# Loading the first two float64 weight tiles ahead of expert 1, and taking the low part of the next rows ahead of the row maximum

## The chip, the cores and the metric

One NeuronCore of a Trainium2 chip runs the whole program in one launch. The metric is the device time of one execution in microseconds (us), the median of three runs. Engines: TensorE (PE, matrix products), VectorE (DVE), ScalarE (ACT), GpSimd (POOL, here it issues the gathers) and SyncE (SP, which here only issues DMAs). Each engine takes its instructions in the order in which they are written; semaphores make one engine wait for another.

## The reference

Attention with softmaxed q and k (B 4, H 8, S 576, D 64) gives x of 2304 rows by 512. A mixture of 8 experts picks two experts for each row. A second MLP with a softmax-gated unit and a layer norm follows.

```python
# experts: for each row, its two best experts e with weight g
h = np.maximum(x[mask] @ w1[e], 0.0)            # 512 -> 1024
out[mask] += g * (h @ w2[e])                    # 1024 -> 512
# second MLP, on the 2304 rows that come out
h = x @ w_in                                    # 512 -> 1024
e = np.exp(h - np.max(h, axis=-1, keepdims=True))
sm = e / (np.sum(e, axis=-1, keepdims=True) + 1e-09)
solu = h * sm
ln = (solu - mu) / np.sqrt(var + 1e-06) * g_ln
return (ln @ w_out).astype(np.float32)          # 1024 -> 512
```

w_in and w_out of the second MLP arrive in float64; everything else is float32.

## The kernel before

Every float32 product is made of three matmuls in a reduced-precision type: each operand is split into a high part (a rounded copy, by ScalarE) and a low part (operand minus high part, by VectorE), and high by high, low by high and high by low are added in PSUM.

**The experts.** Each expert gets 640 slots, five tiles of 128 rows. For one expert `e` the program runs eight blocks `mm1(e, m)`, m = 0 to 7, and then five `mm2(e, a)`. A block of `mm1` is 24 matmuls of 320 columns into one PSUM bank `a`, then one ScalarE instruction (L789, `hh`, the high part of the relu) and one VectorE instruction (L790, `hl`, the low part), which is also the last reader of the bank. There are two banks `a`, so the matmuls of block m wait for `hl` of block m - 2. Between the blocks the program writes, in this order, the weights of the next expert (`load_w1`, L157, on SyncE), the rows of the next expert (gather by GpSimd, L736; store, L741; turned read, L747) and one step of a background job `bg`.

**The background job** is a Python generator, `decode_all`, advanced one step by each `next(bg)`. It turns w_in and w_out from float64 words into float32 on VectorE. Its first step only issues two DMAs (`load_f64(0)`, `load_f64(1)`, L204, 512 KB each, into the buffers X0 and X1). Then each of 16 tiles takes four steps: three VectorE instructions (L212 to L214, the first users of the loaded tile), three (L217 to L219), two (L222, L223), and two with the store of the result and the load of the tile after next. In the expert loop one step is taken at each m from 3 to 7 and at each `mm2`.

**The second MLP** handles 18 tiles of 128 rows in turns i. In each turn TensorE does `h_in(i)` (L894, 48 matmuls into a bank `a`, two banks) and then, except in turns 0, 1 and 4, the output product `o_out` of an earlier tile (L986, 24 matmuls of 512 columns). The rest of a turn stands on VectorE and ScalarE: `solu_max(i)` is the row maximum over the bank (L903, VectorE) and the exponential on ScalarE (L906); `solu(i)` (L912 to L919, VectorE) normalizes and is the bank's last reader; `rstd(i - 1)` is a row of small VectorE and ScalarE instructions (L927 to L937). `x2_turn(i + 2)` brings rows to come into transposed order (L870, VectorE) and has ScalarE make their high part `x2h` (L872); `x2_low` takes the low part `x2l` (L877, VectorE) one turn later. `d_low` (L963, VectorE, from turn 4 on) and `d_turn` (L955 on VectorE, L958 on ScalarE) do the same for the second product; for tile 1 the ScalarE copies L976 do it behind `rstd`. `h_in(i + 1)` needs `x2h` in its first matmul and `x2l` in its fifth.

The whole order is the order of the Python code (the schedule is manual), engine by engine.

Of the kernel before, what the change touches and what calls it, by code (L numbers as in the profile page):

```python
# [22 lines left out]
NC = NT // 128  # L23
# [63 lines left out]
def attn_moe_kernel(ctx: ExitStack, tc: tile.TileContext, q, k, v, w_gate, w_noise, noise,  # L87
# [62 lines left out]
    def load_w1(e, j):  # L150
        t = new_raw([128, KD, 256], F32, "raw")
        src = (win32 if e == E else w1[e])[:, 256 * j:256 * j + 256]
        if e < EQ:
            SP.dma_start(out=t, in_=src.rearrange("(k p) f -> p k f", p=128))
        else:
            for g in range(4):
                SP.dma_start(out=t[32 * g:32 * g + 32], in_=src[128 * g:128 * g + 128].rearrange("(k c) f -> c k f", c=32))  # L157
        raw[1, e, j] = t
# [16 lines left out]
    def split_w2(e, j):  # L175
        t = raw.pop((2, e, j))
        if e < E:
            A.copy(W2h[j], t)
            (pick_engine(24 + j, P, V) if e == 0 else V).tensor_sub(W2l[j], t, W2h[j])
        else:  # L180
            wh, wl = W2h[j], W2l[j]
            if j < 2:
                t2 = slot(("XH", "XL")[j], [128, 2, 2, 512], F32R, "w2x")
                wh, wl = t2[:, 0], t2[:, 1]
            WO.append((wh, wl))
            for i in range(2):
                g = gl[:, 2 * j + i:2 * j + i + 1]
                A.activation(out=wh[:, i, :], in_=t[:, i, :], func=AF.Copy, scale=g)
                V.scalar_tensor_tensor(wl[:, i, :], t[:, i, :], g, wh[:, i, :],
                                       op0=OP.mult, op1=OP.subtract)  # L190
# [10 lines left out]
    def load_f64(i):  # L201
        src, _, rs, c0 = dec_src(i)
        t = slot(("X0", "X1")[i % 2], [128, 1024], U32, "f64")
        SP.dma_start(out=t, in_=src[rs, c0:c0 + 512].bitcast(U32))  # L204
        d64[i] = t

    def decode(i):
        _, dst, rs, c0 = dec_src(i)
        t = d64.pop(i).rearrange("p (c w) -> p c w", w=2)
        lw, hw = t[:, :, 0], t[:, :, 1]  # L210
        a, b, c = (slot(tag, [128, 512], U32, f"dec{j}") for j, tag in enumerate((("S5", "S6")[i % 2], "S7", "S11")))
        V.tensor_scalar(b, hw, 3, 0x3FFFFFF8, op0=OP.logical_shift_left, op1=OP.bitwise_and)  # L212
        V.scalar_tensor_tensor(a, hw, 0xC0000000, b, op0=OP.bitwise_and, op1=OP.bitwise_or)
        V.scalar_tensor_tensor(a, lw, 29, a, op0=OP.logical_shift_right, op1=OP.bitwise_or)  # L214
        yield

        V.tensor_scalar(b, lw, 0x1FFFFFFF, 6, op0=OP.bitwise_and, op1=OP.logical_shift_right)  # L217
        V.tensor_scalar(c, a, 0xFF800000, None, op0=OP.bitwise_and)
        V.tensor_tensor(b, b, c, op=OP.bitwise_or)  # L219
        yield  # L220
        af, bf, cf = (x.bitcast(F32) for x in (a, b, c))
        V.tensor_sub(bf, bf, cf)  # L222
        V.scalar_tensor_tensor(af, bf, 2.0 ** -23, af, op0=OP.mult, op1=OP.add)  # L223
        yield

        V.tensor_scalar(c, hw, 20, 0x7FF, op0=OP.logical_shift_right, op1=OP.bitwise_and)
        V.scalar_tensor_tensor(af, c, 896.5, af, op0=OP.is_ge, op1=OP.mult)
        SP.dma_start(out=dst[rs, c0:c0 + 512], in_=af)

    def decode_all():  # L230
        load_f64(0)
        load_f64(1)
        yield
        for i in range(16):
            yield from decode(i)
            if i < 14:
                load_f64(i + 2)
            yield
# [493 lines left out]
    def gather_x(e, a):  # L732
        c = E * a + e
        t = (new_row if e < EQ else new_hop)([128, DM], F32, "xg")
        first = e == 0 and a < TA
        P.indirect_dma_start(out=t, out_offset=None, in_=xd[0:NRA, :] if first else xd, in_offset=bass.IndirectOffsetOnAxis(  # L736
            ap=idxA[:, a:a + 1] if first else idx[:, c:c + 1], axis=0))
        xg[e, a] = t

    def write_x(e, a):  # L740
        SP.dma_start(out=xs_d[e, a], in_=xg[e, a])  # L741
# [34 lines left out]
    def mm1(e, m):  # L776
        hi, lo = XT[e]
        pa = bank_a()
        j, o = m // 2, 128 * (m % 2)
        for n in range(2):  # L780
            for kk in range(KD):
                wh, wl = W1h[j][:, kk, o:o + 128], W1l[j][:, kk, o:o + 128]
                xh, xl = hi[:, kk, HC * n:HC * n + HC], lo[:, kk, HC * n:HC * n + HC]
                for s, (a, b) in enumerate(((wh, xh), (wh, xl), (wl, xh))):
                    T.matmul(pa[:, n, 0:HC], lhsT=a, rhs=b, start=(kk == 0 and s == 0),  # L785
                             stop=(kk == KD - 1 and s == 2))
        h, l = h_tiles(m)
        h2, l2 = (x.rearrange("p (n c) -> p n c", n=2) for x in (h, l))
        A.activation(out=h2, in_=pa[:, :, 0:HC], func=AF.Relu)  # L789
        V.scalar_tensor_tensor(l2, pa[:, :, 0:HC], 0.0, h2, op0=OP.max, op1=OP.subtract)  # L790
# [68 lines left out]
    def x2_read(t):  # L859
        x = x2r[t] = new_raw([128, 2, DM], F32, "xq")  # L860
        for g in range(4):
            SP.dma_start(out=x[32 * g:32 * g + 32, 0].rearrange("i (b f) -> i b f", b=4),  # L862
                         in_=xx[t].rearrange("(b i) f -> i b f", i=32)[:, :, 128 * g:128 * g + 128])
# [11 lines left out]
    def x2_low(t):  # L875
        hi, lo, xt = x2T[t]
        V.tensor_sub(lo, xt, hi)  # L877
        x2T[t] = (hi, lo)
# [82 lines left out]
    def d_low(t):  # L961
        hi, lo, xt = dT[t]
        V.tensor_sub(lo, xt, hi)  # L963
        dT[t] = (hi, lo)
# [188 lines left out]
    def load_gl():  # L1153
        for g in range(4):
            SP.dma_start(out=gl[32 * g:32 * g + 32], in_=g_ln[256 * g:256 * g + 256].rearrange("(k c) -> c k", c=32))
# [31 lines left out]

    load_gl()
    bg = decode_all()
    for e in range(1, E):  # L1190
        for m in range(KF):
            mm1(e, m)
            if m < 4:
                split_w2(e, m)
                load_w1(e + 1, m)
            if e + 1 < E and m < NA:
                gather_x(e + 1, m)
            if EQ <= e + 1 < E:
                if 1 <= m < NA + 1:
                    write_x(e + 1, m - 1)  # L1200
                if 3 <= m:
                    read_x(e + 1, m - 3)
            if m >= 3:
                next(bg, None)
            if e == 2 and m == 5:
                pair_gates()
                count_overflow()
        if stop:
            return
        for a in range(NA):  # L1210
            if e + 1 < E:
                xt_tile(e + 1, a)
            mm2(e, a)
            if e < E - 1:
                next(bg, None)
                if a < 4:
                    split_w1(e + 1, a)
                    load_w2(e + 1, a)
                continue
            gather_y(a)  # L1220
            if a < 2:
                for j in (2 * a, 2 * a + 1):
                    split_w1(E, j)
                    load_w2(E, j)
            elif a == 2:
                next(bg, None)
                combine(0)
                split_w2(E, 0)
            elif a == 3:
                x2_trans(0)  # L1230
                combine(1)
                split_w2(E, 1)
# [7 lines left out]
    for i in range(NC + 3):  # L1240
        if i < NC:
            h_in(i)
        if i == 1:
            d_trans(0)
        if NP <= i - 1 < NC - 2:
            d_read(i - 1)
        if 1 <= i < NC - 2:
            x2_read(i + 2)
        if i < NC:
            solu_max(i)  # L1250
        if NP <= i - 2 < NC - 2:
            d_low(i - 2)
        if 2 <= i < NC - 1:
            x2_low(i + 1)
        if i < NC:
            solu(i)
        if NP <= i < NC - 2:
            d_write(i)
        if i == 0:
            x2_trans(2)  # L1260
        if i < NC - 3:
            combine(i + 3)
        if i == 1:
            split_w2(E, 3)
        if 1 <= i <= NC:
            rstd(i - 1)
        if 2 <= i < 2 + NP:
            o_out(i - 2)
        if i >= 3 + NP:
            o_out(i - 3)  # L1270
        if i in (NP, NC - 1, NC):
            d_trans(i - 1)
        if NP <= i - 1 < NC - 2:
            d_turn(i - 1)
        if 1 <= i < NC - 2:
            x2_turn(i + 2)
        if i + 5 < NC:
            gather_y(i + 5)
# [31 lines left out]
```

## Time and profile before

| what | value |
|---|---|
| time, median of 3 runs | 799.62 us (799.24 to 801.07) |
| the profiled execution | 799.58 us, of which its span (first to last instruction) 797.8 us |
| TensorE busy | 743.6 us, 93% of the span |
| VectorE / ScalarE / GpSimd busy | 67% / 37% / 18% |
| mean granted TensorE clock | 0.975 of full speed |
| mean DMA rate | 180 GB/s |

The span is divided by time: attention and routing up to some 110 us, expert 0 to 179 us, experts 1 to 7 to 582 us, the second MLP to the end. TensorE is busy nearly throughout from expert 1 on, so its few gaps there, and the stretches at a lower granted clock, are where time can be found or lost. The granted clock has two levels here, 1.00 (2.4 GHz) and 0.50 (1.2 GHz). In a timeline row the bracket tells how long the engine sat idle before the instruction and who ended that.

### The profile page before, as it was taken

The numbers are of one execution on the slowest core, as the hardware profiler recorded it, in microseconds if no ns is written. First come the engines' busy times: TensorE is split into PE (matmuls) and PEld (weight loads), VectorE is DVE, ScalarE is ACT, GpSimd is POOL, SyncE is SP. The second block draws the span as 40 slices with busy tenths as digits, with TensorE's granted clock in tenths as the row PEclk, the third lists the DMA queues.
The fourth block names the chain that finished last, engine by engine and source line by source line (L and its number), as shares of the span: only waits on it lengthen the run. The fifth ranks groups of instructions, "written<-read, shape, count | busy, mean of one in ns | idle before, by whom it ended". The sixth has DMA issues, their size and how long they took to land. (4 is left out here: it accounts for less than half of the span.)

```text
span 797.8 us, 12649 instructions
## 1 busy us (share of the span) xinstructions
PE 743.6 (93%) x4754; PEld 670.1 (84%) x4754; DVE 532.2 (67%) x929; ACT 298.7 (37%) x489; POOL 144.8 (18%) x130
## 2 busy tenths in 40 slices
PE   2877877999699999999999999999999899999997
PEld 1776866989689989889889899899898898899986
DVE  6999784244475876776766766765467878777771
ACT  1556551233033233233233333233345544454441
POOL 3684375100100200201101101000344211100000
PEclk9998799999799999999999999999999999999999
DMA  9973363446745865965847848542747776655411
GB/s 276 280 241 107 120 198 106 146 133 161 207 159 163 241 207 153 267 211 158 251 146 217 245 158 234 176 132 80 211 132 231 233 221 215 192 180 182 149 40 40
DMA packets 115280, 143.60 MB, mean 180 GB/s; under 512 B 19856, under 2 KB 80784, under 8 KB 115216
## 3 DMA queue, kind: packets, MB, share of 16 engines
q1 hardware_dynamic: 109136, 122.83, 50.4%
q0 software_dynamic: 6080, 19.93, 8.9%
q8 instruction: 38, 0.62, 0.3%
q14 instruction: 26, 0.21, 0.1%
HBM read 99.46 MB, written 43.25 MB: 179 GB/s over the span
## 5 line engine op out<-in xcount | busy, mean ns | idle before, releaser
L785 PE MATMUL a<-xh,w1h 128*128 128x320 f32 x448 | 139.9, 312 | 6.9 <-DVE hl L790 6.9
L785 PE MATMUL a<-xl,w1h 128*128 128x320 f32 x448 | 139.6, 312 | 0.0
L785 PE MATMUL a<-xh,w1l 128*128 128x320 f32 x448 | 139.6, 312 | 0.0
L821 PE MATMUL b<-w2h,hl 128*128 128x512 f32 x320 | 126.8, 396 | 0.0
L821 PE MATMUL b<-w2l,hh 128*128 128x512 f32 x320 | 126.4, 395 | 0.0
L821 PE MATMUL b<-w2h,hh 128*128 128x512 f32 x320 | 126.3, 395 | 0.0
L736 POOL DMA_INDIRECT xg<-xd,idx x38 | 39.5, 1040 | 327.7 <-DMA xs<-xg 317.7
L789 ACT ACTIVATE hh<-a 128x640 fp32r<-128x640 f32 x56 | 39.5, 706 | 153.3 <-PE a L785 153.3
L790 DVE SCALAR_TENSOR_TENSOR hl<-a,hh 128x640 fp32r<-128x640 f32 x56 | 46.2, 824 | 74.8 <-ACT hh L789 74.8
L785 PEld LDWEIGHTS a<-xh,w1h 128*128 128x128 f32 x448 | 85.3, 190 | 7.5 <-DVE hl L790 7.1
L785 PEld LDWEIGHTS a<-xl,w1h 128*128 128x128 f32 x448 | 85.3, 190 | 0.4
L785 PEld LDWEIGHTS a<-xh,w1l 128*128 128x128 f32 x448 | 85.2, 190 | 0.0
L821 PEld LDWEIGHTS b<-w2l,hh 128*128 128x128 f32 x320 | 60.1, 188 | 14.1
L821 PEld LDWEIGHTS b<-w2h,hh 128*128 128x128 f32 x320 | 60.2, 188 | 13.8
L821 PEld LDWEIGHTS b<-w2h,hl 128*128 128x128 f32 x320 | 60.0, 188 | 13.9
L844 POOL DMA_INDIRECT yg<-yd,posi x36 | 36.6, 1017 | 166.1 <-DVE w1l L173 72.9
L894 PE MATMUL a<-w1h,x2l 128*128 128x256 f32 x288 | 57.9, 282 | 2.5 <-DVE x2l L877 2.5
L894 PE MATMUL a<-w1h,x2h 128*128 128x256 f32 x288 | 58.1, 283 | 0.7 <-DVEq L1003 0.5
L894 PE MATMUL a<-w1l,x2h 128*128 128x256 f32 x288 | 57.2, 280 | 0.0
L771 ACT CAST xh<-xt 128x512 fp32r<-128x512 f32 x30 | 18.6, 621 | 94.5 <-DVE xt L769 94.5
L986 PE MATMUL b<-w2x,dT 128*128 128x512 f32 x216 | 53.5, 396 | 0.1
L986 PE MATMUL b<-w2h,dT 128*128 128x512 f32 x144 | 48.0, 395 | 0.0
(216 smaller groups left out, 1377.0 us busy)
## 6 DMA issues: line engine op xcount, KB each, us to landing
raw<-in_moe_w_dram SPq DMA_DIRECT2D x40, 512.0 KB, 3.9
raw<-in_moe_w_dram SPq DMA_DIRECT2D x96, 128.0 KB, 3.0
yd<-yo SPq DMA_DIRECT2D x40, 256.0 KB, 2.1
xs<-xg SPq DMA_DIRECT2D x30, 256.0 KB, 4.2
xg<-xs SPq DMA_DIRECT2D x120, 64.0 KB, 4.4
dd<-ed SPq DMA_DIRECT2D x14, 512.0 KB, 2.6
dq<-dd SPq DMA_DIRECT2D x56, 128.0 KB, 3.1
k<-in_k_dram SPq DMA_DIRECT2D x4, 1024.0 KB, 7.0
```

The source lines that it names most:

```text
L736: P.indirect_dma_start(out=t, out_offset=None, in_=xd[0:NRA, :] if first else xd, in_offset=bass.IndirectOffsetOnAxis(ap=idxA[:, a:a + 1] ...
L771: A.copy(hi, x)
L785: T.matmul(pa[:, n, 0:HC], lhsT=a, rhs=b, start=(kk == 0 and s == 0), stop=(kk == KD - 1 and s == 2))
L789: A.activation(out=h2, in_=pa[:, :, 0:HC], func=AF.Relu)
L790: V.scalar_tensor_tensor(l2, pa[:, :, 0:HC], 0.0, h2, op0=OP.max, op1=OP.subtract)
L821: T.matmul(pb, lhsT=x, rhs=y, start=(kk == 0 and s == 0), stop=(kk == KF - 1 and s == 2))
L844: P.indirect_dma_start(out=r, out_offset=None, in_=yd[0:n, :], in_offset=bass.IndirectOffsetOnAxis(ap=posi[:, c, j:j + 1], axis=0))
L894: T.matmul(pa[:, n, 256 * c:256 * c + 256], lhsT=x[:, kk, :], rhs=w[2 * n + c][:, kk, :], start=(kk == 0 and s == 0 and c == 0), stop=(kk ...
L986: T.matmul(pb, lhsT=x[:, kk, :], rhs=w, start=(kk == 0 and s == 0), stop=(kk == KF - 1 and s == 2))
```

## The change

It makes two edits. The first takes the first step of `bg` (the two float64 loads) ahead of the expert loop and leaves out the step at m = 3 of expert 1, so that from m = 4 of expert 1 on every step stands where it stood. The second writes `x2_low(i + 1)` ahead of `solu_max(i)` in the turns of the second MLP; it stood behind `solu_max(i)` and `d_low(i - 2)`.

```diff
     load_gl()
     bg = decode_all()
+    next(bg)
     for e in range(1, E):
...
-            if m >= 3:
+            if m >= 3 + (e == 1):
                 next(bg, None)
...
         if 1 <= i < NC - 2:
             x2_read(i + 2)
+        if 2 <= i < NC - 1:
+            x2_low(i + 1)
         if i < NC:
             solu_max(i)
         if NP <= i - 2 < NC - 2:
             d_low(i - 2)
-        if 2 <= i < NC - 1:
-            x2_low(i + 1)
         if i < NC:
             solu(i)
```

SyncE's instructions, from the end of expert 0 to m = 5 of expert 1, as a difference (f are the float64 tiles, raw the weights of expert 2, xg and xs its rows; a number behind xs_ is the tile).

```order
 L824 DMA yd<-yo 128x512 x3
 L1155 DMA gl<-in_moe_g_ln_dram 32x8x1 x4
+L204 DMA f_1843<-in_moe_w_in_dram 128x1024
+L204 DMA f_1845<-in_moe_w_in_dram 128x1024
 L157 DMA raw<-in_moe_w_dram 32x4x256 x8
 L741 DMA xs_0_95<-xg 128x512
...
 L747 DMA xg<-xs_0_95 32x4x128 x4
-L204 DMA f_1995<-in_moe_w_in_dram 128x1024
-L204 DMA f_1997<-in_moe_w_in_dram 128x1024
 L741 DMA xs_3_98<-xg 128x512
 L747 DMA xg<-xs_1_96 32x4x128 x4
```

The two loads now stand ahead of all weight loads and row transfers of expert 2 that are issued during expert 1.

VectorE's instructions at the start of turn 4 of the second MLP, before (dq and dT are d's tile and its parts, a is the bank of `h_in(4)`):

```order
L955 STREAM_TRANSPOSE dq<-dq 128x4x8x32
L870 STREAM_TRANSPOSE xq<-xq 128x4x4x32
L903 TENSOR_REDUCE col<-a 128x1
L963 TENSOR_TENSOR dT<-dq,dT 128x1024
L877 TENSOR_TENSOR x2l<-xq,x2h 128x512
L912 TENSOR_SCALAR col<-col 128x1
```

And the same place now:

```order
L955 STREAM_TRANSPOSE dq<-dq 128x4x8x32
L870 STREAM_TRANSPOSE xq<-xq 128x4x4x32
L877 TENSOR_TENSOR x2l<-xq,x2h 128x512
L903 TENSOR_REDUCE col<-a 128x1
L963 TENSOR_TENSOR dT<-dq,dT 128x1024
L912 TENSOR_SCALAR col<-col 128x1
```

The subtraction L877 has moved up past the maximum L903 and, from turn 4 on, past L963; in turns 2 and 3 it has moved past L903 alone.

## Rows read from the trace of the kernel before

**Rows 1.** Waits of TensorE: waiting instruction <- releaser: us in total, times, longest.
```profile
PE a L785 <- DVE hl L790: 6.9, 1, 6.9
...
PE a L894 <- DVE x2l L877: 2.5, 2, 2.2
```

**Rows 2.** VectorE's timeline, expert 1: start, us, engine, instruction [idle before].
```profile
196.36 0.82 DVE L790 SCALAR_TENSOR_TENSOR hl<-a,hh 128x640 fp32r<-128x640 f32 x1 [1.36 <-ACT hh L789]
206.81 0.43 DVE L212 TENSOR_SCALAR dec<-f 128x512 uint32<-128x512 uint32 x1 [9.63 <-DMA f<-in_moe_w_in_dram]
...
208.60 0.81 DVE L790 SCALAR_TENSOR_TENSOR hl<-a,hh 128x640 fp32r<-128x640 f32 x1
```

**Rows 3.** SyncE's timeline: DMA issues from the end of expert 0.
```profile
179.03 2.35 SPq L1155 DMA_DIRECT2D gl<-in_moe_g_ln_dram  x4
184.47 5.26 SPq L157 DMA_DIRECT2D raw<-in_moe_w_dram  x8
...
200.70 0.90 SPq L204 DMA_DIRECT2D f<-in_moe_w_in_dram  x2
```

**Rows 4.** TensorE's timeline, the matmul after the wait of expert 1.
```profile
209.47 0.63 PE L785 MATMUL a<-xh,w1h 128*128 128x320 f32 x1 [6.86 <-DVE hl L790]
```

**Rows 5.** Windows: TensorE busy, its granted clock (PEclk), DMA share, GB/s.
```profile
210.00:215.00 5.00, 5.00 (x21) 0.50 0.67 191
```

**Rows 6.** ScalarE's timeline, first matmul of expert 1.
```profile
199.14 0.71 ACT L789 ACTIVATE hh<-a 128x640 fp32r<-128x640 f32 x1 [2.82 <-PE a L785]
202.66 0.70 ACT L789 ACTIVATE hh<-a 128x640 fp32r<-128x640 f32 x1 [2.81 <-PE a L785]
216.01 0.71 ACT L789 ACTIVATE hh<-a 128x640 fp32r<-128x640 f32 x1 [12.64 <-PE a L785]
```

**Rows 7.** TensorE's timeline, turn 5 of the second MLP.
```profile
625.81 0.50 PE L894 MATMUL a<-w1h,x2h 128*128 128x256 f32 x2 [0.16 <-ACT x2h L872]
...
628.70 0.80 PE L894 MATMUL a<-w1h,x2l 128*128 128x256 f32 x2 [2.16 <-DVE x2l L877]
...
635.43 2.96 PE L986 MATMUL b<-w2x,dT 128*128 128x512 f32 x12
```

**Rows 8.** VectorE's timeline, turn 2 of the second MLP.
```profile
606.58 1.19 DVE L903 TENSOR_REDUCE col<-a 128x1 f32<-128x1024 f32 x1
607.68 0.67 DVE L877 TENSOR_TENSOR x2l<-xq,x2h 128x512 fp32r<-128x512 f32 x1
609.03 0.15 DVE L912 TENSOR_SCALAR col<-col 128x1 f32<-128x1 f32 x1 [0.68 <-ACT ed L906]
```

**Rows 9.** ScalarE's timeline, the high part of tiles 3 and 5.
```profile
606.69 0.62 ACT L872 CAST x2h<-xq 128x512 fp32r<-128x512 f32 x1 [1.87 <-DVE xq L870]
...
625.15 0.61 ACT L872 CAST x2h<-xq 128x512 fp32r<-128x512 f32 x1
```

**Rows 10.** VectorE's timeline, turn 4.
```profile
625.69 1.22 DVE L903 TENSOR_REDUCE col<-a 128x1 f32<-128x1024 f32 x1 [0.94 <-PE a L894]
...
627.97 0.68 DVE L877 TENSOR_TENSOR x2l<-xq,x2h 128x512 fp32r<-128x512 f32 x1
```

**Rows 11.** TensorE's timeline, end of turn 3's first matmul.
```profile
613.47 0.40 PE L894 MATMUL a<-w1h,x2l 128*128 128x256 f32 x2
```

**Rows 12.** The chain that ended last, in order of time: start, us, what.
```profile
614.00 6.10 PE b L986 x24
620.09 5.58 PE a L894 x48
...
646.72 5.55 PE b L986 x24
```

**Rows 13.** TensorE's timeline, a wait of expert 0.
```profile
117.30 0.39 PE L809 MATMUL a<-xh,w1h 128*128 128x256 f32 x1 [2.05 <-DVE hl L812]
```

**Rows 14.** VectorE's timeline, turn 6.
```profile
646.75 1.23 DVE L903 TENSOR_REDUCE col<-a 128x1 f32<-128x1024 f32 x1 [1.78 <-PE a L894]
```

**Rows 15.** ScalarE's timeline, the high part of tile 7.
```profile
645.37 0.62 ACT L872 CAST x2h<-xq 128x512 fp32r<-128x512 f32 x1
```

## Prediction

> **What bounds the kernel now.** The table of the profile says that TensorE is busy for 93% of the span, so I read first what it waits for. The view of waits, TensorE alone, has two entries behind expert 0 that are worth a microsecond [rows 1]: once 6.9 us in the experts' first product, for VectorE's `hl`, and 2.5 us in two pieces in the second MLP, for `x2l`. The reader should see the counts: these are single events and no steady cost. What the one event is made of stands in the timelines of that place. The lower level of the granted clock shows in windows, and the chain that ended last shows that from 635 us on there is only TensorE, one `h_in` and one `o_out` in turn, so that a microsecond won ahead of that point is won at the end.
>
> The first event: VectorE finishes `hl` of block 4 at 197.2 us, then sits idle for 9.63 us at the background job's first instruction, because the float64 tile has not landed [rows 2]. SyncE issued that load only at 200.70 [rows 3], behind the weights and rows of expert 2. The `hl` of block 5 stands behind the waiting instruction in VectorE's order and comes at 208.60 [rows 2], so the bank for block 7 is not free and TensorE waits 6.86 us [rows 4]. After the wait the granted clock is 0.50, the lower of its two levels [rows 5], so the block runs slowly too.
>
> **The first edit, step by step.** It adds nothing: the same two loads, earlier. SyncE is done with the small loads L1155 at 181.4 and issues nothing until 184.47, where the weight loads wait for their buffers [rows 3]. The two issues take 0.90 us, so they fit in that gap and push nothing back. The first tile was needed 6.1 us after its issue last time (200.70 to 206.81) [rows 2, 3]; from about 181.5 that gives 187.6, or 193 at double the time, and VectorE asks for it at 197.2. So the wait of 9.63 us goes completely. Moving 1 MB out of the busiest stretch also cannot hurt the row transfers that are issued there.
>
> What is late next? In the place of the wait VectorE has the first decoding step, 1.8 us (206.81 to 208.60), ending at 199.0, and `hh` of block 5 starts at 199.14 [rows 2, 6]. `hl` of block 5 then ends near 200.7, ahead of block 7's start at about 202.5. So TensorE doesn't wait at all. Blocks come 3.52 us apart (199.14 to 202.66), so `hh` of block 7 moves from 216.01 to 202.66 + 3.52 = 206.18 [rows 6]. **That is 9.83 us**: 6.86 of waiting, and 2.97 of a block at the lower clock. Behind it, the transposes of expert 2's rows come 10 us sooner, yet their turned reads are issued from 198 us on and get ahead of the need by more than they did, and the other background steps move with TensorE. I take the whole 9.83; the lower bound, if only the idle time counted, is 6.86, the upper one 9.83.
>
> **The second edit, step by step.** It adds no instruction; it moves a subtraction of 0.67 us [rows 8]. The place aimed at is turn 4: `x2h` of tile 5 is ready at 625.76 [rows 9], but `x2l` only starts at 627.97, behind the maximum (which waits for `h_in(4)`) and `d_low` [rows 10]. TensorE waits 2.16 us for it and runs slowly afterwards: `h_in(5)` takes from 625.81 to 635.43 [rows 7], 9.62 us, against 5.58 in [rows 12]. Taken alone, with `x2l` done at 626.45, it would lose only some 0.2 us and end at 631.6: a gain of 3.8.
>
> But in turns 2 and 3 the move costs VectorE time, and there VectorE, not TensorE, sets the pace. In turn 2 the maximum starts at 606.58, `x2l` fills the time in which ScalarE makes the exponential, and L912 comes at 609.03, 2.45 us after the maximum's start, still with 0.68 idle ahead of it [rows 8]. So `x2l` is free today. Now it stands first and must wait for `x2h`, which ScalarE ends at 607.31 [rows 9]; it runs from 607.34 to 608.0, the maximum starts there and L912 follows 2.45 us later. Turn 2 becomes 1.4 us later: 0.7 of waiting, 0.7 of a subtraction that has lost its cover. Turn 3 has the same instructions in the same relation, and loses another 1.4. (If `x2h` were ready in time, each would lose 0.67: the other bound.)
>
> What hangs on that? `rstd(1)`, then ScalarE's dT copies, then `o_out(1)`: from 614.00 to 615.4 [rows 12]. TensorE has nothing ahead of it, as `h_in(3)` is done at about 613.9 [rows 11]. `o_out(1)` and `h_in(4)` take 6.1 and 5.6 [rows 12], to 627.1. `x2h` of tile 5 comes 2.8 late, 625.15 becoming 627.95, and ends at 628.56 [rows 9]; `x2l` follows at once, to 629.3. `h_in(5)` starts at 628.6, needs the low part after four matmuls, waits 0.2, and has 44 matmuls left. At full clock those take 5.58 x 44 / 48 = 5.12 us, so it ends at 634.4 instead of 635.43 [rows 7, 12]. **The second edit gives 1.0 us**, not 3.8: the wait of 2.16 for `x2l` is largely replaced by a wait of 1.5 for `x2h`.
>
> Afterwards VectorE must not become the bound. From turn 6 on it sat idle for 1.78 us ahead of the maximum [rows 14], which began at 646.75; it was therefore done with the transpose at 644.97. `x2h` ends at 645.99 [rows 15], so 1.02 of waiting and some 0.6 for the subtraction (to the next issue) fit into the 1.78. Behind the maximum the subtraction's place is saved in part. So TensorE keeps its pace, and VectorE works off what it is late.
>
> **Sum.** 799.58 (the profiled execution, 0.04 below the median) - 9.83 - 1.0 = 788.75, say 788.8.
>
> **The clock in the ramp.** The new plan leaves TensorE idle for about 1.5 us twice (613.9 to 615.4, 627.1 to 628.6). Today a wait of 2.16 us in turn 5 ended with slow matmuls: 44 of them took 628.70 to 635.43, 6.73 us [rows 7], 1.6 more than the 5.12; but a wait of 2.05 us in expert 0 was followed by a matmul of 0.39 us, hardly slower than later ones [rows 13]. So the rows allow both. A fall in the first gap costs nothing, since it only fills the second one; one in the second gap costs up to 1.6. By the Trainium skill (TensorE: Matmul & The Clock Gate, What's actually happening), the array returns to the half clock when it has not been busy, and how many matmuls that slows varies from run to run. That would speak for the rival below, 790.4; the rows above show it once and deny it once, so I keep it as a rival.
>
> **Rivals.**
> 1. The clock falls in the second gap. `h_in(5)` then ends at 629.3 + 6.73 = 636.0, 0.6 later than now: 799.58 - 9.83 + 0.6 = 790.4.
> 2. The ramp hides the subtraction's new place (`x2h` ready, or the maximum waiting for TensorE anyway). Then the second edit gives between 2.6 (0.67 lost in each turn) and 3.8: 786.0 to 787.1. Against it: the maximum of turn 2 shows no idle time ahead of it [rows 8].
> 3. The first stall is only passed on: VectorE waits for expert 2's rows instead, and part of the 9.83 is lost, down to 6.86 or less: 791.7 to 797. For it: DMA is busy there, 0.67 in [rows 5]. Against it: SyncE issues that stretch's transfers no later than before.
> 4. Slower: the second edit puts VectorE's turn over TensorE's 11.1 us (5.6 + 5.6 [rows 12]) in the steady turns. From the point where `x2h` comes more than 0.2 us later than in [rows 15] and the saving behind the maximum doesn't make up for it, every turn pays; to eat both gains (10.8 us) the 12 turns behind would have to pay 0.9 us each; at 1.0 the time is 788.8 + 12 = 800.8. Against it: 1.78 against 1.62.
> 5. The loads don't come sooner, because the DMAs ahead of them hold SyncE: no change, 799.6 less at most 1.
>
> **How the numbers follow.** The forecast has 0.55 (788 to 789.6), rival 1 0.20, rival 2 0.10, rival 3 0.08, rival 5 0.03, rival 4 0.04. The range 786.0 to 791.5 holds the first three and the best of the fourth, and takes in both bounds of the turn's cost. About 0.2% (1.6 us) is what a measurement of this kernel can tell from no change; the forecast and rivals 1 to 3 lie beyond it: faster 0.93, the same 0.03, slower 0.04.
>
> **What would show it.** The loads L204 at about 181.5; no VectorE idle at L212 in expert 1; TensorE without the wait at block 7, clock 1.00 throughout; `mm2` of expert 1 starting at 206 instead of 215.8. In the second MLP, about 10 us earlier than now: idle time ahead of `x2l` in turns 2 and 3, the maximum 1.4 later in turn 2; `o_out(1)` waiting 1.5 us; `h_in(5)` waiting for `x2h` rather than `x2l`, and ending about 10.8 us ahead of 635.43. Wrong would be: a wait for the rows of expert 2 on TensorE, or waits in every turn behind turn 6.

## The result, and the profile after

The changed kernel takes **789.56 us** (median of 4 runs, 788.43 to 790.55) where the kernel before took 799.43 on the same chip (4 runs, 797.77 to 801.07): a ratio of 0.9876 [0.985, 0.9903], 9.9 us less. 788.8 was predicted. The profiled execution takes 790.4 us, its span 788.6.

**The loads.** SyncE's timeline around the end of expert 0 (start, us, instruction):

```profile
180.42 2.31 SPq L1155 DMA_DIRECT2D gl<-in_moe_g_ln_dram  x4
182.78 0.92 SPq L204 DMA_DIRECT2D f<-in_moe_w_in_dram  x2
185.86 5.26 SPq L157 DMA_DIRECT2D raw<-in_moe_w_dram  x8
```

The two loads stand right behind L1155, 15.7 us ahead of the step that first needs them. The weights come at 185.86 where they came at 184.47 [rows 3]. That is 1.39 us later, but so is everything: the first `hh` of expert 1 starts at 182.93 and started at 181.54. The loads push nothing back. VectorE's timeline, where the wait of 9.63 us stood [rows 2]:

```profile
197.75 0.82 DVE L790 SCALAR_TENSOR_TENSOR hl<-a,hh 128x640 fp32r<-128x640 f32 x1 [1.36 <-ACT hh L789]
198.49 0.49 DVE L212 TENSOR_SCALAR dec<-f 128x512 uint32<-128x512 uint32 x1
...
201.27 0.82 DVE L790 SCALAR_TENSOR_TENSOR hl<-a,hh 128x640 fp32r<-128x640 f32 x1 [0.84 <-ACT hh L789]
```

L212 follows with no idle time, and `hl` of block 5 now waits for ScalarE, so VectorE has time left. ScalarE's timeline, the last three `hh` of expert 1:

```profile
200.53 0.71 ACT L789 ACTIVATE hh<-a 128x640 fp32r<-128x640 f32 x1 [2.81 <-PE a L785]
204.05 0.70 ACT L789 ACTIVATE hh<-a 128x640 fp32r<-128x640 f32 x1 [2.81 <-PE a L785]
207.57 0.70 ACT L789 ACTIVATE hh<-a 128x640 fp32r<-128x640 f32 x1 [2.82 <-PE a L785]
```

Blocks come 3.52 us apart to the end; the last two stood 13.35 apart [rows 6]. The windows (TensorE busy, PEclk, DMA share, GB/s at the end of the row) show TensorE without a gap and at full clock in expert 1, and at full clock to the end:

```profile
176.00:216.00 40.00, 40.00 (x245) 37.70 (x244) 21.08 (x29) 11.55 (x15) 4.70 (x5) 1.00 0.84 228
...
570.00:788.00 218.00, 210.28 (x1349) 188.26 (x1347) 153.90 (x308) 101.63 (x190) 31.66 (x30) 1.00 0.53 166
```

**The second MLP.** VectorE in turns 2, 3 and 4 (`x2l` L877, the maximum L903, L912):

```profile
598.98 0.71 DVE L877 TENSOR_TENSOR x2l<-xq,x2h 128x512 fp32r<-128x512 f32 x1 [0.69 <-ACT x2h L872]
599.61 1.21 DVE L903 TENSOR_REDUCE col<-a 128x1 f32<-128x1024 f32 x1
602.09 0.15 DVE L912 TENSOR_SCALAR col<-col 128x1 f32<-128x1 f32 x1 [1.27 <-ACT ed L906]
...
609.62 0.69 DVE L877 TENSOR_TENSOR x2l<-xq,x2h 128x512 fp32r<-128x512 f32 x1 [0.69 <-ACT x2h L872]
610.23 1.22 DVE L903 TENSOR_REDUCE col<-a 128x1 f32<-128x1024 f32 x1
...
620.24 0.69 DVE L877 TENSOR_TENSOR x2l<-xq,x2h 128x512 fp32r<-128x512 f32 x1 [1.04 <-ACT x2h L872]
620.85 1.22 DVE L903 TENSOR_REDUCE col<-a 128x1 f32<-128x1024 f32 x1
```

In turn 2 VectorE stands idle for 0.69 us ahead of `x2l`, which then runs ahead of the maximum, and the idle time ahead of L912 has grown from 0.68 [rows 8] to 1.27: the subtraction has lost its cover. I count from the start of `h_in(0)`, 582.85 before and 574.43 now. The maximum of turn 2 moves from 23.73 to 25.18, that of turn 3 to 35.80 from 32.96: 1.45 and then another 1.39 late. TensorE's timeline shows what hangs on it:

```profile
607.05 3.30 PE L986 MATMUL b<-w2x,dT 128*128 128x512 f32 x12 [0.53 <-ACT dT L976]
...
620.26 0.51 PE L894 MATMUL a<-w1h,x2h 128*128 128x256 f32 x2 [1.56 <-ACT x2h L872]
...
620.99 0.51 PE L894 MATMUL a<-w1h,x2l 128*128 128x256 f32 x2
...
626.26 2.96 PE L986 MATMUL b<-w2x,dT 128*128 128x512 f32 x12
```

`h_in(5)` waits 1.56 us for `x2h` and hardly for `x2l` any more (2.16 in [rows 7]), and `o_out(2)` starts 51.83 us behind `h_in(0)`; before it was 52.58 (635.43 - 582.85). So the edit won 0.75 us there. In the view of TensorE's waits (us in total, times, longest) L785 has no row, and the second MLP's products have these, beside 0.5 us ahead of `h_in(0)` that was there before too:

```profile
PE a L894 <- ACT x2h L872: 1.6, 1, 1.6
PE b L986 <- issue: 1.3, 2, 0.9
...
PE b L986 <- ACT dT L976: 0.5, 1, 0.5
```

The wait for `hl` (6.9) and that for `x2l` (2.5) of [rows 1] are gone.

**Where the time went, in one sum.** The spans differ by 9.2 us (797.8 - 788.6). From the first `hh` of expert 1 to that of its last block it is 34.47 before and 24.64 now, 9.83 less; from there to `h_in(0)` 366.84 and 366.86, the same; from `h_in(0)` to the end 214.95 and 214.17, 0.78 less; and up to expert 1, which the change doesn't touch, 1.39 more. 9.83 + 0.78 - 1.39 = 9.22.

### The profile page after: what moved, and what is told of

Same layout as the page of the kernel before. It is cut to its first block, busy times and chain, and to the rows that moved or that the text cites. A ratio compares the mean times of both kernels' runs of the same rounds, so it can differ in the third digit from the quotient of the medians.

```text
span 788.6 us, 12651 instructions
## 1 busy us (share of the span) xinstructions
PE 742.2 (94%) x4754; PEld 668.5 (85%) x4754; DVE 531.4 (67%) x929; ACT 298.9 (38%) x489; POOL 145.2 (18%) x130
## 5 line engine op out<-in xcount | busy, mean ns | idle before, releaser
L785 PE MATMUL a<-xh,w1h 128*128 128x320 f32 x448 | 138.6, 309 | 0.0
L785 PE MATMUL a<-xh,w1l 128*128 128x320 f32 x448 | 138.5, 309 | 0.0
L785 PE MATMUL a<-xl,w1h 128*128 128x320 f32 x448 | 138.5, 309 | 0.0
L785 PEld LDWEIGHTS a<-xl,w1h 128*128 128x128 f32 x448 | 84.2, 188 | 0.4
L785 PEld LDWEIGHTS a<-xh,w1h 128*128 128x128 f32 x448 | 84.2, 188 | 0.3
L785 PEld LDWEIGHTS a<-xh,w1l 128*128 128x128 f32 x448 | 84.3, 188 | 0.0
L986 PEld LDWEIGHTS b<-w2x,dT 128*128 128x128 f32 x216 | 39.3, 188 | 10.8 <-issue 1.8
```

Source lines behind the costliest of these rows:

```text
L986: T.matmul(pb, lhsT=x[:, kk, :], rhs=w, start=(kk == 0 and s == 0), stop=(kk == KF - 1 and s == 2))
```

## The experiments

The runs are in three groups, each on one chip with its own runs of the kernel before: the first four of the table behind the kernels shown, the next four, and the last two. Because the part ahead of expert 1 differs by up to 3.2 us from one execution to the next, the profiles are compared by the two stretches of that sum: **A**, first to last `hh` of expert 1's first product, and **B**, `h_in(0)` to the end. The stretch between them is 366.84 to 366.88 us in all twelve profiles. The medians of the kernel before in the three groups are 796.26, 796.98 and 798.25 us; the two rows "before again" are single executions.

| kernel | A | B | time, us | ratio to before |
|---|---|---|---|---|
| before, as shown | 34.47 | 214.95 | | |
| after, as shown | 24.64 | 214.17 | 789.56 | 0.9876 [0.985, 0.9903] |
| loads alone | 24.64 | 213.53 | 788.81 | 0.9908 [0.9883, 0.9934] |
| low part alone | 34.59 | 213.87 | 796.53 | 1.0002 [0.9985, 1.0018] |
| early place from turn 4 | 24.63 | 211.41 | 785.25 | 0.9867 [0.984, 0.9893] |
| before, wait filled | 31.38 | 214.67 | 795.14 | 0.9981 [0.9964, 0.9998] |
| early place in turns 2, 3 | 24.64 | 219.51 | 792.83 | 0.9933 [0.9908, 0.9958] |
| loads at m = 2 | 24.64 | 214.67 | 789.61 | 0.9905 [0.9877, 0.9933] |
| before again | 32.46 | 215.04 | 796.11 | |
| before again | 33.26 | 213.29 | 796.09 | |
| after again | 24.63 | 214.34 | 789.85 | 0.9876 [0.984, 0.9912] |
| early place in turn 4 alone | 24.63 | 214.26 | 787.37 | 0.9841 [0.9805, 0.9876] |

The theory is the prediction's: the loads give 9.83 us, the moved subtraction wins 3.8 in turn 4 and pays 2.8 in turns 2 and 3. The rivals are that turns 2 and 3 pay nothing, and that a part of the first gain is the clock's and not the wait's.

**The first edit alone.**

```diff
     bg = decode_all()
+    next(bg)
...
-            if m >= 3:
+            if m >= 3 + (e == 1):
```

> The two early loads alone, the subtraction where it was. Theory of the prediction: 9.83 us less than before, 789.8, and in the second MLP the same waits as before, 2.16 us for x2l in turn 5 with slow matmuls behind it. Rival (the second edit is what gains, or the first stall is passed on): less than 8 us gained, with a new wait on TensorE between block 7 of expert 1 and expert 2.

A is 24.64, as in the changed kernel, so the whole of A's gain is this edit's. By time it gives 7.45 us (796.26, 23 runs, to 788.81, 6 runs); its interval, 5.3 to 9.3 us, does not reach 9.83. It is less than the 8 us that the rival named, but the rival's sign, a new wait of TensorE, isn't there: the stretch behind A is 366.87. A second thing was not expected. The chain that ended last has `h_in(5)`'s last 44 matmuls behind the same wait of 2.16 us for `x2l`:

```profile
618.45 5.44 PE a L894 x44
```

They take 5.44 us, at full clock, where the same chain of the kernel before has 6.89. The wait was the same to 0.01 us, and the clock did not fall.

**The second edit alone.**

```diff
         if 1 <= i < NC - 2:
             x2_read(i + 2)
+        if 2 <= i < NC - 1:
+            x2_low(i + 1)
         if i < NC:
             solu_max(i)
...
-        if 2 <= i < NC - 1:
-            x2_low(i + 1)
```

> The early subtraction alone, the loads where they were. Theory: 0.75 to 1.0 us less than before, 798.6 to 798.9; the maximum of turn 2 starts 1.4 us later against h_in(0) than before, that of turn 3 2.7 later, and h_in(5) waits about 1.6 us for x2h instead of 2.2 for x2l. Rival (the ramp hides the new place of the subtraction, and what held the second edit back was something of the shifted program, such as the pause in o_out(0)): 2.6 to 3.8 us less, 795.8 to 797.

The time doesn't change: 796.53 against 796.26, 1.0002 [0.9985, 1.0018], between 1.2 us won and 1.4 lost. The mechanism is there all the same. VectorE's timeline of turn 2:

```profile
607.34 0.69 DVE L877 TENSOR_TENSOR x2l<-xq,x2h 128x512 fp32r<-128x512 f32 x1 [0.69 <-ACT x2h L872]
607.95 1.22 DVE L903 TENSOR_REDUCE col<-a 128x1 f32<-128x1024 f32 x1
```

and TensorE's waits:

```profile
PE a L785 <- DVE hl L790: 7.4, 1, 7.4
PE b L986 <- ACT dT L976: 1.8, 1, 1.8
PE a L894 <- ACT x2h L872: 1.6, 1, 1.6
```

The prediction's two waits of 1.5 us are these 1.8 and 1.6. In the changed kernel the first is only 0.5, because there TensorE had already lost 1.3 us in front of it ("issue" in its view of waits; more on that below).

**Early from turn 4 on, old place in turns 2 and 3** (both edits, without the part of the second that should cost).

```diff
+        if 4 <= i < NC - 1:
+            x2_low(i + 1)
         if i < NC:
             solu_max(i)
         if NP <= i - 2 < NC - 2:
             d_low(i - 2)
-        if 2 <= i < NC - 1:
+        if 2 <= i < 4:
             x2_low(i + 1)
```

> Both edits, but the subtraction goes ahead of the maximum only from turn 4 on; in turns 2 and 3 it stands behind it as before. Theory (turns 2 and 3 each lose 1.4 us and eat most of the 3.8 that turn 4 gains): 3.8 us less than with the loads alone, 786.0, with h_in(5) waiting less than 0.5 us in all and the clock at 1.00 there. Rival (the early place costs in turn 4 and after, not in turns 2 and 3): the time of the changed kernel or more, 788.8 and above.

This is the fastest of its group, 785.25 us (5 runs, 784.87 to 786.31), 3.6 less than the loads alone (787.02 to 790.11); the runs of the two don't overlap. B is 211.41: 3.54 less than in the profile of the kernel before, against 3.8 in the prediction, and 2.76 less than in that of the changed kernel, against 2.8. Both are differences between two executions, and against the profile of the loads alone, where the clock did not fall, it is 2.12. TensorE has one wait for `x2l` in the second MLP, and its timeline shows where:

```profile
597.71 0.51 PE L894 MATMUL a<-w1h,x2l 128*128 128x256 f32 x2 [0.33 <-DVE x2l L877]
```

That is `h_in(3)`, where the kernel before waited 0.30 us too (the smaller of the two pieces of 2.5 in [rows 1]). In `h_in(5)` no wait is left in the view. VectorE, turn 2 and turn 4:

```profile
595.88 1.19 DVE L903 TENSOR_REDUCE col<-a 128x1 f32<-128x1024 f32 x1
596.98 0.67 DVE L877 TENSOR_TENSOR x2l<-xq,x2h 128x512 fp32r<-128x512 f32 x1
...
615.08 0.69 DVE L877 TENSOR_TENSOR x2l<-xq,x2h 128x512 fp32r<-128x512 f32 x1 [1.04 <-ACT x2h L872]
615.69 1.21 DVE L903 TENSOR_REDUCE col<-a 128x1 f32<-128x1024 f32 x1
```

In turn 2 the maximum covers `x2h`'s 0.69 us and ScalarE's exponential covers the subtraction; in turn 4 `x2l` is first and delays nothing on which TensorE waits.

**The kernel before, with matmuls in the wait.** 46 matmuls on old operands, into a bank that nobody reads, ahead of block 7: the wait stays, only the clock is kept up.

```diff
+    def fill(n):
+        ps, x = bank_t(), XT[1][0]
+        for _ in range(n):
+            T.matmul(ps[:, 0:HC], lhsT=W1h[0][:, 0, 0:128], rhs=x[:, 0, 0:HC], start=True, stop=True)
...
+            if e == 1 and m == 7:
+                fill(46)
             mm1(e, m)
```

> The kernel before, with 46 added matmuls of 320 columns (6.75 us at full clock) into an unused bank ahead of block 7 of expert 1, so that TensorE is busy while VectorE waits for the float64 tile. They compute nothing that is read. Theory (the slow block is TensorE's own idling): granted clock 1.00 through block 7, which takes 3.5 us instead of 6.4; the time falls by 2.97 us at most, to 796.7, although work was added. Rival (the clock falls there for another reason, such as the busy DMA queues): block 7 stays slow, and the time is 799.6 or a little more.

TensorE's timeline and the window of the stretch (PEclk third from the end):

```profile
201.82 6.91 PE L1193 MATMUL t<-xh,w1h 128*128 128x320 f32 x46
```

```profile
180.00:216.00 36.00, 36.00 (x237) 35.28 (x237) 17.43 (x23) 9.77 (x13) 4.73 (x5) 1.00 0.72 200
```

Block 7 ran at full clock and A fell by 3.09 us, so the slow block went with TensorE's idling, and 6.74 us beyond the 24.64 were left, the wait with the added matmuls in it. By time it gave 1.1 us (0.2 to 2.9 by the interval): less than 2.97, but the interval takes in 2.3, the mean slow block of the four profiles below. In this execution the clock fell in turn 5 (44 matmuls in 6.93 us), as before.

The loads alone and this run both gave less than the profile before had promised. How much do wait and slow block vary, then, from one execution of the kernel before to the next? **The kernel before, twice more, unchanged:**

> The kernel before once more, for its profile. If the clock behind a wait varies from run to run, the wait of block 7 is 6 to 7.5 us again, while the slow part of block 7 costs anything between 0.5 and 3 us and h_in(5) takes 7.9 us (full clock behind the wait for x2l) or 9.6. If it does not vary, block 7 ends 9.8 us late and h_in(5) takes 9.6 again.

> The kernel before a third time, for the same two readings as the second.

TensorE behind the wait in the first, and the window behind it:

```profile
207.39 0.64 PE L785 MATMUL a<-xh,w1h 128*128 128x320 f32 x1 [6.28 <-DVE hl L790]
```

```profile
208.00:210.00 2.00, 2.00 (x10) 2.00 (x9) 1.97 (x4) 0.00 (x0) 1.05 (x2) 0.50 0.34 96
210.00:212.00 2.00, 2.00 (x15) 2.00 (x15) 0.75 (x2) 0.00 (x0) 0.88 (x1) 0.94 0.88 226
```

and in the second:

```profile
208.46 0.63 PE L785 MATMUL a<-xh,w1h 128*128 128x320 f32 x1 [6.41 <-DVE hl L790]
```

```profile
210.00:212.00 2.00, 2.00 (x9) 2.00 (x9) 1.82 (x3) 0.00 (x0) 1.67 (x2) 0.50 0.63 136
212.00:214.00 2.00, 2.00 (x13) 2.00 (x12) 0.00 (x0) 0.00 (x0) 0.04 (x1) 0.80 0.94 245
```

The wait is 6.28 and 6.41, but the clock comes back some 3 us behind its end in the one and some 4 in the other, where [rows 5] show it low for at least the 5 us to 215. A beyond the 24.64 without the wait is 7.82 and 8.62. With the 9.83 of [rows 6] and the 9.95 of the low part alone, four profiles give 7.8 to 10.0, 9.06 in the mean, of which the slow block is 1.5 to 3.0. The execution on which the prediction was built had the largest slow block of the four. In turn 5, too, the clock fell in one of the two (B 215.04) and not in the other (213.29).

**The early place in turns 2 and 3 alone** (loads early, `2 <= i < 4` ahead of `solu_max`, the rest at the old place), to measure their cost by itself.

> The loads early, and the subtraction ahead of the maximum in turns 2 and 3 alone; from turn 4 on behind maximum and d_low as before. Theory (turns 2 and 3 lose 1.3 to 1.4 us each, and turn 4 gains): x2l of turn 4 starts 2.0 us later against h_in(0) than with the loads alone, TensorE loses 1.6 us ahead of h_in(5) for x2h and 1.4 inside it for x2l; from h_in(0) to o_out(2) 53 us, against 51.3 measured with the loads alone and 49.2 with the early place from turn 4 on. Rival (the early place costs nothing in turns 2 and 3): 51.3.

`o_out(2)` starts 57.14 us behind `h_in(0)`, later than either theory expected, and the time is 792.83. The same reading gives 51.16 with the loads alone and 49.01 with the early place from turn 4 on. TensorE's timeline, and VectorE's maximum of turn 4:

```profile
590.84 0.29 PE L894 MATMUL a<-w1l,x2h 128*128 128x256 f32 x1 [0.81 <-issue]
...
621.07 0.79 PE L894 MATMUL a<-w1h,x2l 128*128 128x256 f32 x2 [2.47 <-DVE x2l L877]
```

```profile
618.06 1.23 DVE L903 TENSOR_REDUCE col<-a 128x1 f32<-128x1024 f32 x1 [1.26 <-issue]
```

The wait for `x2l` of turn 4 is 2.47 us now and is followed by slow matmuls (44 in 8.1 us). But TensorE also paused in `h_in(2)` with no releaser, and `o_out(0)` starts 2.8 us later than in the kernels without such a pause (21.04 behind `h_in(0)` against 18.16 to 18.23). That reached `x2l` as well: VectorE stood idle for 1.26 us ahead of the maximum of turn 4, which began when the late `h_in(4)` ended. `x2l` started 48.34 us behind `h_in(0)`, 3.20 later than with the loads alone (45.14); take off the 1.26, and an estimate of 1.94 is left, where the theory said 2.0. How much of the 57.14 is the pause's is not measured, so the run gives the sign of the cost, and its size only by that estimate.

**The loads one block earlier only** (the step at m = 3 taken at m = 2), to see how early is early enough.

```diff
-            if m >= 3:
+            if m >= 3 + (e == 1) or (e == 1 and m == 2):
```

> The two loads one block earlier than before, at m = 2 of expert 1 instead of m = 3, and no second edit. Theory (the stall follows the landing of the float64 tile one for one): the issue moves from 200.7 to about 197.2, the wait of TensorE from 6.86 to 3.4 us, and with or without slow matmuls behind it the time is 3.5 to 6.5 us less than before. Rival (the stall is set by the queue of row transfers, in which the loads only change places): the wait stays at 6 us or more.

SyncE's timeline, and then VectorE's:

```profile
194.14 0.97 SPq L204 DMA_DIRECT2D f<-in_moe_w_in_dram  x2
```

```profile
199.87 0.43 DVE L212 TENSOR_SCALAR dec<-f 128x512 uint32<-128x512 uint32 x1 [2.31 <-DMA f<-in_moe_w_in_dram]
```

A miss on the place: the issue came at 194.14, since in SyncE's order it stands ahead of the transfers of m = 3. The tile lands at 199.87, and VectorE waits 2.31 us for it, but TensorE not at all (A 24.64). So it is not necessary that VectorE's wait goes: the bank has at least that much to spare. The ratio is that of the loads alone (0.9905 and 0.9908).

**The changed kernel again, and the early place in turn 4 alone** (`i == 4`; all other turns old), on a third chip. The first run asks what the second edit adds to the loads, the second whether the steady turns need it.

> The changed kernel again, beside the next one on one chip. Theory as the runs so far leave it (the second edit ends h_in(5) at a fixed 51.5 to 52 us after h_in(0), where the old order ends it at 51.2 or 52.6 as the clock falls or not): the time within 1 us of the loads alone, a ratio to before near 0.990; h_in(0) to the end 213.9 to 214.2 us. Rival (the second edit gains the 1.0 us of the prediction on top in every run): 0.9865 to 0.988.

> The loads early and the subtraction ahead of the maximum in turn 4 alone, in all other turns behind it. Theory (turn 4 is the only place where the early subtraction is worth anything): h_in(0) to the end 211.4 us as with the early place from turn 4 on, 2.2 to 2.8 us less than the changed kernel, ratio to before near 0.986. Rival (the steady turns need the early place too): more than 212 us from h_in(0) to the end, with waits for x2l behind turn 5.

The changed kernel gives 0.9876 [0.984, 0.9912], which holds both answers: not settled by time. B is 214.34, a little above what was expected. Turn 4 alone has 0.9841 [0.9805, 0.9876]; its interval overlaps that of "from turn 4 on", so these two are not told apart either. By the medians it is 2.5 us faster than the changed kernel beside it (787.37 and 789.85), as expected, but the runs overlap. Its waits in the second MLP, and the window behind the first of them (PEclk third from the end):

```profile
PE b L986 <- issue: 2.2, 3, 1.0
...
PE a L894 <- issue: 0.3, 1, 0.3
```

```profile
598.00:600.00 2.00, 2.00 (x7) 0.50 0.23 71
```

B was expected at 211.4 and is 214.26 in this profile. The 2.2 us of pause in `o_out(0)` and the slow matmuls behind it are 2.20 of the difference: `o_out(2)` starts 51.21 us behind `h_in(0)`, against 49.01 with the early place from turn 4 on. Most of the rest, 0.6 us, is the row of 0.3, which the view gives no releaser. It is the fifth matmul of `h_in(6)`, the first to need `x2l` of tile 6, and VectorE's subtraction had ended 0.06 us ahead of it:

```profile
632.17 0.51 PE L894 MATMUL a<-w1h,x2l 128*128 128x256 f32 x2 [0.32 <-issue]
```

```profile
631.43 0.68 DVE L877 TENSOR_TENSOR x2l<-xq,x2h 128x512 fp32r<-128x512 f32 x1
```

So turn 5, with its subtraction at the old place, was late by 0.3 us in this execution, as the rival says. Behind it no matmul waits for `x2l` or `x2h`: the turns from 6 on don't need the early place.

## Why the prediction was right, and which term was off

- **The wait for the tile, and what takes its place:** right. The wait is gone, nothing is late next, `hh` of block 7 comes 9.83 us sooner, and the stretch up to the second MLP is unchanged to 0.04 us in every profile. The rivals that it would be passed on (3) or that the loads would not come sooner (5) are refuted.
- **The size of the first term:** 9.83 was one execution's. The wait of 6.86 was 6.3 to 7.4 in four profiles, and the 2.97 of slow block was 1.5 to 3.0. The mean of the four is 9.06; the loads alone measured 7.45 [5.3, 9.3] by time, which holds 9.06 and not 9.83.
- **Turns 2 and 3, 1.4 us each:** right, 1.45 and 1.39. That the first turns hide the subtraction's new place (rival 2) is refuted by the profiles of the changed kernel and of the low part alone: `x2l` waits 0.69 for `x2h` with the maximum behind it.
- **Turn 4, 3.8 alone and 1.0 net:** right as a mechanism: 3.54 alone, 2.76 paid, 0.78 net against the execution that it was worked out from. `h_in(5)` starts 45.83 us behind `h_in(0)`; 45.75 was forecast.
- **The step that failed** is the price of the old wait in turn 5: "`h_in(5)` takes from 625.81 to 635.43 [rows 7], 9.62 us" was taken as what it costs always. In six profiles that have the old order in turn 4 with no pause ahead, the clock fell behind that wait in four (B 214.67, 214.67, 214.95, 215.04) and not in two (213.29, 213.53); the mean is 214.36. The three profiles with the second edit, two of them with a pause that the last section tells of, have 213.87, 214.17 and 214.34, mean 214.13. So **the second edit gives 0.2 us by these means, where 1.0 was predicted**: 0.7 won (214.83 - 214.13) when the clock would have fallen, 0.7 lost (213.41) when it would not. With six and three profiles the 0.2 is not clear of nothing. The timed run of that edit alone (1.0002) agrees, though its interval just holds a gain of 1.0 us. A part of the spread is another wait: in eight of the twelve profiles VectorE waited 0.2 to 0.4 us ahead of L870 in turn 2 (0.35 before, 0.41 in the changed kernel). In the four where it did not, B is 214.67 and 214.67 with the clock fallen and 213.29 without in the old order, and 213.87 with the second edit alone: 0.8 won or 0.6 lost.
- **The clock in the second gap (rival 1):** it stayed up behind the 1.56 us of the changed kernel and the 1.58 of the low part alone. The Trainium skill (TensorE: Matmul & The Clock Gate, What's actually happening) says that how many matmuls come slow varies between runs of one kernel; the rows agree and go further: behind 2.14 to 2.16 us of idle the 44 matmuls took 6.89 to 6.97 us in four executions, and 5.44 and 5.46, with no fall of the clock, in two.
- **VectorE in the steady turns (rival 4):** refuted. The subtraction waits 1.04 or 1.05 us for `x2h` in each (1.02 forecast), and no matmul waits behind turn 5.
- **The total** came out closer than its terms: 9.06 + 0.23 = 9.3 by the profiles' means, 10.8 predicted, 9.9 measured with an interval from 7.7 to 12.0. The two edits timed each alone add up to less still, 7.45 - 0.27 = 7.2. So that the time came within 0.8 us of the forecast is in part luck. The profiled 790.4 lies above its sum because the part ahead of expert 1 took 1.39 us more in that execution.

## What to carry to other kernels

A subtraction that stands behind another engine's wait is free where it is; moving it up is worth it only in the turns where somebody waits for it, so split such a change by turns: early from turn 4 on has a B 2.76 us below that of the changed kernel. The two were not timed on one chip, and their ratios (0.9867 and 0.9876) don't tell them apart; timed beside the loads alone it is 3.6 us faster. Background work that waits for its own load blocks everything that is written behind it on that engine, so issue the load ahead of the queue's long stretch; some 7 us sooner, counted from expert 1's first `hh`, was already enough here. A wait that ends in slow matmuls has a price that differs between executions: take it from several profiles of the kernel before, not from one.

## What the runs showed of the hardware

- **The clock behind one and the same wait.** The wait of TensorE in turn 5, 2.14 to 2.16 us in six profiles, was followed by the low clock in four of them. Matmuls that compute nothing, put into a wait, made the whole program faster by a little (0.9981 [0.9964, 0.9998]).
- **A pause with no releaser.** In 4 of the 12 profiles (the changed kernel twice, the early place in turns 2 and 3, and in turn 4 alone) TensorE paused for 1.3 to 2.4 us in all, 18 to 23 us behind `h_in(0)`, with one matmul or pair every 0.7 to 1.4 us. Behind it the clock fell to 0.50 in the last two and stayed at 1.00 in the two of the changed kernel. TensorE's timeline of the changed kernel's second profile:

```profile
594.50 0.28 PE L894 MATMUL a<-w1l,x2h 128*128 128x256 f32 x1 [1.08 <-issue]
595.23 0.28 PE L894 MATMUL a<-w1h,x2l 128*128 128x256 f32 x1 [0.45 <-issue]
595.95 0.37 PE L894 MATMUL a<-w1h,x2l 128*128 128x256 f32 x1 [0.44 <-issue]
```

The DMA engines are nearly full there: their share is 0.92 and 0.86 in the two windows of 2 us from 594 us in the changed kernel. That doesn't tell these profiles from others, for it is 0.97 and 0.83 at the same place (from 593 us) with the loads at m = 2, which has no pause. The queue of GpSimd's gathers (packets, MB, share of 16 engines), from 588 to 598 us in the changed kernel, with a pause,

```profile
q0 software_dynamic: 572, 1.86, 61.5%
```

and from 587 to 597 us with the loads at m = 2, without one:

```profile
q0 software_dynamic: 573, 1.86, 61.1%
```

The two queues that load instructions moved one packet each in both windows, so that doesn't tell them apart either. The cause stays open; no run was made for it. In the changed kernel it cost nothing of its own, since the wait for `dT` behind it became shorter by as much (0.5 against 1.8).
